# First phase of an attention and gated-layer kernel: weights made without ScalarE, and five of eight w3 row tiles moved into the first gated layer

## The chip, the cores and the metric

The kernel runs on one core of a Trainium2 chip. A core has TensorE (matrix products, PE in the profile; its weight loads are PEld), VectorE (DVE), ScalarE (ACT), GpSimd (POOL) and SyncE (SP), whose queue issues all DMA transfers here. The metric is device time in microseconds (us): the median of several runs. Less is better. One profiled execution gives the trace that the rows below come from.

## What is computed

```python
attn_out = sigmoid(q @ k.T / sqrt(64) - log(448)) @ v     # 4 batches, 12 heads, 448 rows, 64 columns
x = attn_out as (1792, 768)
xn = x / rms(x) * rms_g
x  = (silu(xn @ w_gate) * (xn @ w_val)) @ w_out           # first gated layer, width 1536
y  = ((x @ w1) * (x @ w2)) @ w3 @ w_out2                  # second layer, width 1024
```

The weights arrive as 64-bit floats. On the chip each is turned into a 32-bit float and then split into a rounded high part and the rest (both in TensorE's fp32r format), so that every large product is three matmuls.

## The kernel before

**Attention.** The 12 heads of a batch are worked in 6 pairs; pairs 0 to 11 (batches 0 and 1) make up the first phase, and pairs 12 to 23 are spread through the layers that follow. `load_pair` brings one pair's rows (q, k and v, 736 KB, tile `raw`, 3 buffers), `scores` makes the four score blocks of a pair and applies the sigmoid on ScalarE (tiles `a` and `al`), `attend` multiplies with v into `av`, and `take_out` copies the result to `xr` on ScalarE, writes it to DRAM, squares it on ScalarE and adds the square to `acc` on GpSimd. In the order of TensorE's instructions, pair i's scores stand between the products of pair i-1.

**Weights.** `load_double` brings a 64-bit tile (`wd`). `to_float` decodes it: `mag` is the high word without its sign (ScalarE, L96), VectorE clamps it (L97), shifts it (L98), and joins sign and low word (L106, L109) to the float `wf`. `split_weight` copies `wf` to the high part on ScalarE (L115) and subtracts on GpSimd (L116). Two sets of weights are made in the first phase: the eight tiles of the last weight, w_out2, which stay on chip as `o0` to `o7` (`load_wo2`, `decode_wo2`, one per pair), and the first row tiles of w3. Class `Weights` holds all others in one sequence; at most two loaded tiles (`wd`, 2 buffers) wait for decoding, two decoded ones (`wf`, 2 buffers) for splitting, and four split ones (`ws`) for TensorE.

**w3 @ w_out2.** `w3o_group(kt, nh)` makes one half of one row tile of this product, 24 matmuls of 384 columns, and writes it to DRAM through `w3ot`. Before the change all 8 row tiles (16 groups, 16 weight tiles of 512 columns) are made between the first 12 pairs and the first gated layer. Meanwhile `rms_norm(b)` makes the factor `r` of a batch, and `split_x(b, k)` reads x back from DRAM, scales it (`xs`, L385) and splits it (`x`, ScalarE L262, VectorE L263).

**First gated layer.** For each of 12 column tiles m and both batches, `a_group` makes the gate product and the value product: 18 matmuls of 448 columns each, into one of three PSUM tiles `psm`. The gate's sigmoid is on ScalarE, the two multiplications by it are on VectorE (L491, L495), and they free the PSUM tiles. Two weight tiles of 768 columns (wg and wv) are needed per m. A scheduler in the framework sets the order of each engine's queue once, before the run; within a queue the order is fixed, so an instruction that waits holds all behind it. All DMAs stand in SyncE's queue.

Of the kernel before, what the change touches and what calls it, by code (L numbers as in the profile page):

```python
# [8 lines left out]
F32 = mybir.dt.float32  # L9
# [27 lines left out]
def fused_kernel(ctx: ExitStack, tc: tile.TileContext, qkv, wg, wv, wo, w1, w2, w3, wo2, gam, out):  # L37
# [80 lines left out]
    class Weights:  # L118
# [57 lines left out]

        def split_to(self, n, flush=False):

            n = min(n, len(self.seq) - 1)
            while self.n_split <= n and len(self.split) < self.BUFS:  # L180
# [5 lines left out]
                if double:  # L186
                    f = to_float(f, w)
# [7 lines left out]
                if kt is None:  # L195
                    for j in range(2):
                        split_weight(t[:, :, j * WH : (j + 1) * WH], next(self.blocks), WH)
                elif double:
                    self.late = (i, t, f, w)
                else:  # L200
                    split_weight(t, f, w)
                    self.out -= 1
            if flush:
                self.finish()

# [15 lines left out]
    W = Weights()  # L221
    i_w3 = [[W.add(w3[kt][:, 4 * h : 4 * h + 4, :], 4, True) for h in range(2)] for kt in range(KF2)]
    kept = {}
# [11 lines left out]
    B_ORDER = [0, 3, 1, 4, 2, 5]  # L235
    i_a = [[add_moe(n, w, m) for n, w in (("wg", wg), ("wv", wv))] for m in range(KF1)]
    i_b = {m: [add_moe("wo", wo, m, h) for h in range(2)] for m in range(KD)}
# [59 lines left out]

    A1 = dict(raw=3, a=5, al=2, xr=2, wd=2)
    A2 = dict(raw=2, a=3, al=2, xr=2)
# [6 lines left out]
    xd = {}  # L306

    def load_pair(p):
        if p < NP:
            t = raw[p] = at([P, RAWW], F32, "raw")  # L310

            cuts = (0, S + P, V0, RAWW) if p == 0 else (0, RAWW)
            for c, d in zip(cuts, cuts[1:]):
                nc.sync.dma_start(out=t[:, c:d], in_=qkv[p // HP, p % HP][:, c:d])

# [29 lines left out]
    def take_out(p):  # L345
# [36 lines left out]
    def load_x(b, k):  # L382
        x = scratch("xs")
        nc.sync.dma_start(out=x, in_=xd.pop((b, k)))
        nc.vector.scalar_tensor_tensor(  # L385
            out=x, in0=x, scalar=g_sb[:, k : k + 1], in1=rms[b], op0=ALU.mult, op1=ALU.mult
        )
        return x

    def split_x(b, k):  # L390
        t = x_tile("x", b % 2)
        split2(t, load_x(b, k))
        acts["x", b % 2, k] = t

# [65 lines left out]
    def a_winograd(m):  # L460
        def done(b, g, v):
# [9 lines left out]
    def c_winograd(m):  # L471
        def done(b, x, y):
            nc.vector.tensor_tensor(out=y, in0=x, in1=y, op=ALU.mult)
            acts["ab", b, m] = t = h_tile("ab")
            split2(t, y)

        winograd(i_c2, m, done)


    def h_tile(name):  # L480
        return pools["h"].tile([P, 2, S], F32R, tag="h", bufs=2 * KF1, name=name)

    half = {}

    def a_group(m, b, which):
# [25 lines left out]
    def c_group(m, b, which):  # L511
# [6 lines left out]
        else:  # L518
            s = half.pop((m, b))
            nc.vector.tensor_tensor(out=s, in0=ps, in1=s, op=ALU.mult)  # L520
            t = h_tile("ab")
            split2(t, s)
# [42 lines left out]
    load_pair(0)  # L565
    load_wo2(0)
    load_pair(1)
    load_wo2(1)
    load_pair(2)
    for i in range(NA + 1):  # L570
        if i < NA:
# [3 lines left out]
        if i:  # L575
            attend(i - 1, (3, 0))
        if i < KF2:
            decode_wo2(i)
            load_wo2(i + 2)
# [7 lines left out]
        if i >= KF2 - 1:  # L587
            W.load_to(i - KF2 + 2)
            W.split_to(i - KF2)
        if i == HP:  # L590
            rms_norm(0)
        if i > HP and i - HP <= KD:
            split_x(0, i - HP - 1)


    groups = [(kt, nh) for kt in range(KF2) for nh in range(2)]
    for n, g in enumerate(groups):
        w3o_group(*g)
        W.split_to(n + 4)
        if n == 1:  # L600
            rms_norm(1)
        if n > 3 and n - 4 < KD:
            split_x(1, n - 4)
    att["pool"].release()
    wo2p.release()
    att["pool"], att["bufs"] = pool("att2", "left"), A2
    pools["h"] = pool("h", "right")

# [13 lines left out]

    steps = [lambda: (load_pair(NA), load_pair(NA + 1))]
    for p in range(NA, NP):
# [3 lines left out]
    steps += [lambda: first_half(NP), lambda: None, lambda: rms_norm(B - 1)]  # L628
    units = list(first_units())
    total = sum(u[1] for u in units)  # L630
    spent, n = 0.0, len(steps)
    for u in units:
        spent += run(u)
        while steps and (n - len(steps)) < n * spent / total:
            steps.pop(0)()
    assert not steps
# [21 lines left out]
    pools["xw"].release()  # L658
    pools["h"].release()
    for p in (r1b, wp, scr, r1a, cst, ps_w, ps_av, ps_m, dram):  # L660
        p.release()
# [53 lines left out]
```

## Time and profile before

| what | value |
| --- | --- |
| median of 3 runs | 1138.17 us (1137.58 to 1139.41) |
| the profiled execution's own time | 1137.84 us |
| its span, first to last instruction | 1136.1 us |
| TensorE busy | 1101.1 us (97%) |
| VectorE, ScalarE, GpSimd busy | 643.5, 471.8, 371.8 us |
| mean granted TensorE clock | 0.991 of full speed |

The span is what the rows are measured in; 1.7 us of the execution's own time lie around it. A busy time of VectorE or GpSimd includes time in which an instruction has started and is held. Matmuls are pipelined: the duration of one is longer than the distance to the next, so the pace is read from starts.

### The profile page before, as it was taken

How to read it: one execution, taken by the hardware profiler on the slowest of the kernel's cores; microseconds unless marked ns; L12 is line 12 of the kernel's file. 1: busy time of each engine (PE TensorE's matmuls, PEld its weight loads, DVE VectorE, ACT ScalarE, POOL GpSimd, SP SyncE). 2: the span in 40 equal slices, each digit the busy share in tenths (PEclk: the TensorE clock that was granted, in tenths of full speed). 3: DMA queues.
4: the chain of work that ended last, by engine and by line, in shares of the span. 5: the costliest groups of instructions: out<-in, count | busy, mean ns of one | idle time of the engine just before them, and what ended most of it. 6: DMA issues, size and time to landing. Idle time of an engine off the chain costs nothing.

```text
span 1136.1 us, 13921 instructions
## 1 busy us (share of the span) xinstructions
PE 1101.1 (97%) x5204; PEld 904.1 (80%) x5204; DVE 643.5 (57%) x873; ACT 471.8 (42%) x768; POOL 371.8 (33%) x276
## 2 busy tenths in 40 slices
PE   7779997899999999999999999999999999999998
PEld 2223997777887788787778899999889999899997
DVE  5662677764656565343544365599999222777600
ACT  6766443444344443434433233544443233433321
POOL 2421232121222222131212213556565222556420
PEclk9889999999999999999999999999999999999999
DMA  8554556544344453644433225211112110121131
GB/s 285 193 189 136 170 187 234 192 160 160 133 153 171 148 179 106 201 153 167 161 125 126 93 88 165 102 56 56 56 56 86 55 56 19 56 69 44 38 103 51
DMA packets 55218, 141.41 MB, mean 124 GB/s; under 512 B 5232, under 2 KB 28912, under 8 KB 55152
## 3 DMA queue, kind: packets, MB, share of 16 engines
q1 hardware_dynamic: 55152, 140.53, 36.6%
q8 instruction: 41, 0.67, 0.2%
q14 instruction: 25, 0.20, 0.1%
HBM read 105.91 MB, written 34.60 MB: 124 GB/s over the span
## 4 chain that ended last, share of the span: by engine, by line
PE 84%; DVE 7%; DMA 4%; ACT 2%; issue 1%; POOL 1%; SPq 0%; DVEq 0%; ACTq 0%; POOLq 0%
PE psm L247 17%; PE psm L248 16%; PE psm L249 16%; PE w L247 8%; PE w L248 7%; PE w L249 7%; PE av L343 4%; PE sc L325 4%; DMA wd<-in_wg 2%; DVE wf L106 2%; DVE wf L109 2%; PE psm L328 1%; PE av L339 1%; DVE wf L98 1%; DVE mag L97 1%
## 5 line engine op out<-in xcount | busy, mean ns | idle before, releaser
L116 POOL TENSOR_TENSOR ws<-wf,ws 128x768 fp32r<-128x768 f32 (+1 forms) x104 | 173.9, 1674 | 489.6 <-ACT ws L115 459.4
L247 PE MATMUL w<-w,ws 128*128 128x448 f32 x420 | 154.8, 369 | 1.5 <-ACT w L262 1.5
L248 PE MATMUL w<-w,ws 128*128 128x448 f32 x420 | 154.4, 368 | 0.0
L249 PE MATMUL w<-w,ws 128*128 128x448 f32 x420 | 154.0, 367 | 0.0
L96 ACT ACTIVATE mag<-wd 128x768 f32<-128x768 f32 (+1 forms) x76 | 65.6, 863 | 173.5 <-DVE wf L98 73.5
L247 PE MATMUL psm<-x,ws 128*128 128x448 f32 x288 | 109.4, 380 | 9.5 <-ACT w3ot L292 5.7
L98 DVE TENSOR_SCALAR wf<-mag 128x768 uint32<-128x768 uint32 (+1 forms) x76 | 45.5, 598 | 111.4 <-POOL ws L116 109.2
L116 POOL TENSOR_TENSOR ws<-wd,ws 128x384 fp32r<-128x384 f32 x80 | 87.7, 1112 | 60.8 <-ACT ws L115 60.8
L247 PE MATMUL psm<-hm,ws 128*128 128x448 f32 x288 | 107.4, 373 | 0.0
L248 PE MATMUL psm<-x,ws 128*128 128x448 f32 x288 | 106.2, 369 | 0.0
L249 PE MATMUL psm<-x,ws 128*128 128x448 f32 x288 | 106.0, 368 | 0.0
L115 ACT ACTIVATE ws<-wf 128x768 fp32r<-128x768 f32 (+1 forms) x104 | 78.7, 758 | 65.5 <-PE psm L249 43.4
L248 PE MATMUL psm<-hm,ws 128*128 128x448 f32 x288 | 105.6, 367 | 0.0
L249 PE MATMUL psm<-hm,ws 128*128 128x448 f32 x288 | 104.8, 364 | 0.0
L116 POOL TENSOR_TENSOR ws<-s,ws 128x384 fp32r<-128x384 f32 x60 | 71.1, 1189 | 63.8 <-ACT ws L115 62.1
L325 PE MATMUL sc<-raw 64*128 64x448 f32 x288 | 73.6, 603 | 14.9 <-DMA raw<-in_qkv 9.0
L247 PEld LDWEIGHTS w<-w,ws 128*128 128x128 f32 x420 | 78.7, 188 | 10.9 <-ACT w L262 1.8
L109 DVE SCALAR_TENSOR_TENSOR wf<-wd,wf 128x768 uint32<-128x768 uint32 (+1 forms) x76 | 85.4, 1123 | 1.4
L97 DVE TENSOR_SCALAR mag<-mag 128x768 f32<-128x768 f32 (+1 forms) x76 | 44.3, 583 | 73.7 <-ACT mag L96 73.7
L106 DVE SCALAR_TENSOR_TENSOR wf<-wd,wf 128x768 uint32<-128x768 uint32 (+1 forms) x76 | 84.4, 1110 | 2.5
L249 PEld LDWEIGHTS w<-w,ws 128*128 128x128 f32 x420 | 78.9, 188 | 7.7
L248 PEld LDWEIGHTS w<-w,ws 128*128 128x128 f32 x420 | 78.8, 188 | 7.3
(118 smaller groups left out, 2160.2 us busy)
## 6 DMA issues: line engine op xcount, KB each, us to landing
raw<-in_qkv SPq DMA_DIRECT2D x23, 736.0 KB, 5.3
wd<-in_wo SPq DMA_DIRECT2D x20, 768.0 KB, 5.2
wd<-in_w SPq DMA_DIRECT2D x16, 768.0 KB, 4.5
wd<-in_wg SPq DMA_DIRECT2D x12, 768.0 KB, 4.6
wd<-in_wv SPq DMA_DIRECT2D x12, 768.0 KB, 5.5
wd<-in_w SPq DMA_DIRECT2D x16, 512.0 KB, 4.0
w<-wf SPq DMA_DIRECT2D x16, 384.0 KB, 2.5
wf<-w3o SPq DMA_DIRECT2D x24, 256.0 KB, 2.8
```

Source lines behind the costliest of these rows:

```text
L96: nc.scalar.activation(mag, hi.bitcast(F32), AF.Abs)
L97: nc.vector.tensor_scalar(out=mag, in0=mag, scalar1=HI_MIN, scalar2=HI_MAX, op0=ALU.max, op1=ALU.min)
L98: nc.vector.tensor_scalar(out=u, in0=mag.bitcast(U32), scalar1=3, scalar2=0x3FFFFFFF, op0=ALU.logical_shift_left, op1=ALU.bitwise_and,)
L106: nc.vector.scalar_tensor_tensor(out=u, in0=hi, scalar=0xC0000000, in1=u, op0=ALU.bitwise_and, op1=ALU.bitwise_or)
L109: nc.vector.scalar_tensor_tensor(out=u, in0=lo, scalar=29, in1=u, op0=ALU.logical_shift_right, op1=ALU.bitwise_or)
L115: nc.scalar.activation(t[:, 0, :w], f[:, :w], AF.Copy)
L116: nc.gpsimd.tensor_tensor(out=t[:, 1, :w], in0=f[:, :w], in1=t[:, 0, :w], op=ALU.subtract)
L247: nc.tensor.matmul(ps, wl, xt[:, 0, :], start=first, stop=False)
L248: nc.tensor.matmul(ps, wh, xt[:, 1, :], start=False, stop=False)
L249: nc.tensor.matmul(ps, wh, xt[:, 0, :], start=False, stop=last)
L325: nc.tensor.matmul(ps[:, j, :], r[d, k], r[d, Q0 : Q0 + S], start=True, stop=True)
L343: nc.tensor.matmul(av[p][d, :], r[:, v + j * D : v + (j + 1) * D], a[:, j, :], start=False, stop=(c == 2))
```

## The change

- The eight tiles of w_out2 and the first six half tiles of w3 are decoded and split without ScalarE: `mag` is made on VectorE (a bitwise AND, one more VectorE operation per tile), and the high part on GpSimd (a copy, CAST, one more GpSimd operation per tile).
- Loads of these weights stand behind the load of the next pair's rows in SyncE's queue (`issue_after`), and each decode comes at the end of its pair, one pair later than before.
- x of batches 0 and 1 stays on chip (8 buffers of `xr`): 12 writes to DRAM and 12 reads fall away. `split_x` works one tile ahead.
- Only row tiles 0 to 2 of w3 @ w_out2 come between the 12 pairs and the gated layer. Row tiles 3 to 7 follow the first five column tiles m of the gated layer, one each, and the weight sequence is ordered to match. The second half's attention begins after m = 5.

```diff
+W3_FIRST = 3
...
-    def to_float(raw, w):
+    def to_float(raw, w, scalar=True):
...
-        nc.scalar.activation(mag, hi.bitcast(F32), AF.Abs)
+        if scalar:
+            nc.scalar.activation(mag, hi.bitcast(F32), AF.Abs)
+        else:
+            nc.vector.tensor_scalar(
+                out=mag.bitcast(U32), in0=hi, scalar1=0x7FFFFFFF, scalar2=None, op0=ALU.bitwise_and
+            )
...
-    def split_weight(t, f, w):
-        nc.scalar.activation(t[:, 0, :w], f[:, :w], AF.Copy)
+    def split_weight(t, f, w, scalar=True):
+        if scalar:
+            nc.scalar.activation(t[:, 0, :w], f[:, :w], AF.Copy)
+        else:
+            nc.gpsimd.tensor_copy(out=t[:, 0, :w], in_=f[:, :w])
...
+                    f = to_float(f, w, i >= 2 * W3_FIRST)
...
+    for kt in range(W3_FIRST):
+        add_w3(kt)
+    for m in range(KF1):
+        i_a.append([add_moe(n, w, m) for n, w in (("wg", wg), ("wv", wv))])
+        if W3_FIRST + m < KF2:
+            add_w3(W3_FIRST + m)
...
     def decode_wo2(j):
-        f = to_float(raw2.pop(j), DM)
-        W.finish()
+        f = to_float(raw2.pop(j), DM, False)
         t = wo2p.tile([P, 2, DM], F32R, tag=f"o{j}", name=f"o{j}")
-        W.late = (None, t, f, DM)
+        split_weight(t, f, DM, False)
         o2.append(t)
...
-    A1 = dict(raw=3, a=5, al=2, xr=2, wd=2)
+    A1 = dict(raw=3, a=5, al=2, xr=8, wd=2)
...
-        d = xd[b, h] = dram.tile([P, S], F32, name=f"x{b}_{h}")
-        nc.sync.dma_start(out=d, in_=x)
+        if p < NA:
+            xd[b, h] = x
+        else:
+            d = xd[b, h] = dram.tile([P, S], F32, name=f"x{b}_{h}")
+            nc.sync.dma_start(out=d, in_=x)
...
+    DECODE = {1: 0, 2: 1, 3: 2, 4: 3, 5: 4, 6: 5, 7: 6, 8: 7}
+    W3_AT = {6: 0, 8: 1, 9: 2, 10: 3, 11: 4, 12: 5}
...
+        with tc.issue_after(last_raw[0]):
+            if i in DECODE:
+                decode_wo2(DECODE[i])
+                load_wo2(DECODE[i] + 2)
+            if i in W3_AT:
+                W.load_to(W3_AT[i] + 1)
+                W.split_to(W3_AT[i] - 1)
...
+    def w3o_groups(kt):
+        for nh in range(2):
+            w3o_group(kt, nh)
+            W.split_to(i_w3[kt][1] + 2 + nh)
+            W.load_to(i_w3[kt][1] + 4 + nh)
+
+    w3o_groups(0)
+    rms_norm(1)
+    for k in range(KD + 1):
+        if k % 3 == 2:
+            w3o_groups(k // 3 + 1)
+        split_x(1, k)
...
+    half_a = 4 * (KF1 // 2)
+    for j, u in enumerate(units[:half_a]):
+        run(u)
+        if j % 4 == 3 and len(i_w3) > W3_FIRST + j // 4:
+            w3o_groups(W3_FIRST + j // 4)
```

On ScalarE, these rows before the change stand in the third pair of the first phase (L96 and L115 are the weights' two operations, L330 the sigmoids, L349 the copy of a pair's result):

```order
L330 ACTIVATE a_222<-sc_221,bias_s_88 128x896
L96 ACTIVATE mag_256<-wd_184 128x768
L349 ACTIVATE xr_230<-av_205 128x448
L115 ACTIVATE o1_218<-wf_210 128x768
L354 ACTIVATE acc_234<-xr_230 128x448
L330 ACTIVATE a_239<-sc_238,bias_s_88 128x896
L330 ACTIVATE a_244<-sc_243,bias_s_88 128x896
L330 ACTIVATE al_249<-psm_248,bias_s_88 128x448
L96 ACTIVATE mag_304<-wd_219 128x768
L115 ACTIVATE o2_265<-wf_257 128x768
L330 ACTIVATE a_269<-sc_268,bias_s_88 128x896
```

The same place of ScalarE's queue in the changed kernel (L349 is the sigmoid there, L368 the copy, L376 and L379 the squares):

```order
L349 ACTIVATE a_200<-sc_199,bias_s_88 128x896
L368 ACTIVATE xr_208<-av_195 128x448
L376 ACTIVATE acc_210<-xr_208 128x448
L349 ACTIVATE a_227<-sc_226,bias_s_88 128x896
L349 ACTIVATE a_232<-sc_231,bias_s_88 128x896
L349 ACTIVATE al_237<-psm_236,bias_s_88 128x448
L349 ACTIVATE a_245<-sc_244,bias_s_88 128x896
```

The weights' rows are gone from ScalarE's queue between the sigmoids.

On GpSimd, before the change, the first phase begins with (o0, o1, ... are the tiles of w_out2, acc the sum of squares):

```order
L116 TENSOR_TENSOR o0_183<-wf_177,o0_183 128x768
L116 TENSOR_TENSOR o1_218<-wf_210,o1_218 128x768
L116 TENSOR_TENSOR o2_265<-wf_257,o2_265 128x768
L116 TENSOR_TENSOR o3_313<-wf_305,o3_313 128x768
L358 TENSOR_TENSOR acc_234<-acc_234,sq_281 128x448
L116 TENSOR_TENSOR o4_361<-wf_353,o4_361 128x768
```

In the changed kernel GpSimd has at the same place:

```order
L126 CAST o0_221<-wf_215 128x768
L127 ISA
L127 TENSOR_TENSOR o0_221<-wf_215,o0_221 128x768
L126 CAST o1_267<-wf_261 128x768
L127 TENSOR_TENSOR o1_267<-wf_261,o1_267 128x768
L380 TENSOR_TENSOR acc_210<-acc_210,sq_255 128x448
L126 CAST o2_313<-wf_307 128x768
L127 TENSOR_TENSOR o2_313<-wf_307,o2_313 128x768
```

Each tile now has a CAST ahead of its subtraction, and the sum of squares of pair 1 stands behind the split of tile 1, that of pair 2 behind tile 2.

On VectorE, the changed kernel reaches the first gate multiplication (L521, which frees the first PSUM tile of the gated layer) in this order; the rows ahead of it are the last halves of a w3 tile (mag_1115, wf_1116), the last x tiles of batch 1 (xs, x) and the whole decode of the second wg tile (mag_1152, wf_1153):

```order
L105 TENSOR_SCALAR mag_1115<-mag_1115 128x512
L281 TENSOR_TENSOR x_1012<-xs_924,x_1012 128x448
L410 SCALAR_TENSOR_TENSOR xs_1010<-xr_731,g_sb_86,r_817 128x448
L106 TENSOR_SCALAR wf_1116<-mag_1115 128x512
L114 SCALAR_TENSOR_TENSOR wf_1116<-wd_968,wf_1116 128x512
L281 TENSOR_TENSOR x_1015<-xs_1010,x_1015 128x448
L117 SCALAR_TENSOR_TENSOR wf_1116<-wd_968,wf_1116 128x512
L105 TENSOR_SCALAR mag_1152<-mag_1152 128x768
L106 TENSOR_SCALAR wf_1153<-mag_1152 128x768
L114 SCALAR_TENSOR_TENSOR wf_1153<-wd_1008,wf_1153 128x768
L117 SCALAR_TENSOR_TENSOR wf_1153<-wd_1008,wf_1153 128x768
L521 TENSOR_TENSOR s_1041<-psm_1022,s_1041 128x448
```

Before the change the rows ahead of the first gate multiplication are decodes of wg and wv alone, since x and w3 are done by then:

```order
L97 TENSOR_SCALAR mag_1627<-mag_1627 128x768
L98 TENSOR_SCALAR wf_1628<-mag_1627 128x768
L106 SCALAR_TENSOR_TENSOR wf_1628<-wd_1521,wf_1628 128x768
L109 SCALAR_TENSOR_TENSOR wf_1628<-wd_1521,wf_1628 128x768
L491 TENSOR_TENSOR s_1491<-psm_1472,s_1491 128x448
```

The work on x and on w3 that used to lie ahead of the gated layer now shares VectorE's queue with its first column tile.

## Rows read from the trace of the kernel before

**Rows 1.** First line of the profile's page.
```profile
span 1136.1 us, 13921 instructions
```

**Rows 2.** Busy time by stage: stretch, length, then each engine's busy us, clock, DMA.
```profile
17.90:85.00 67.10, 52.58 (x172) 16.52 (x170) 47.71 (x52) 45.80 (x63) 26.85 (x17) 0.87 0.61 210
85.00:113.20 28.20, 28.05 (x114) 9.23 (x112) 6.59 (x11) 19.68 (x29) 3.40 (x3) 1.00 0.42 137
113.20:184.80 71.60, 71.28 (x402) 67.90 (x400) 49.23 (x69) 29.07 (x51) 21.30 (x15) 1.00 0.57 187
184.80:230.00 45.20, 35.77 (x159) 29.34 (x159) 31.31 (x37) 19.20 (x27) 10.99 (x6) 0.96 0.58 197
230.00:1136.10 906.10, 901.13 (x4323) 777.00 (x4321) 502.36 (x694) 347.38 (x587) 308.07 (x231) 1.00 0.32 106
```

**Rows 3.** Timeline of TensorE: start, us, instruction; starts of pairs and of w3 @ w_out2.
```profile
17.94 1.77 PE L325 MATMUL sc<-raw 64*128 64x448 f32 x8
...
85.04 1.77 PE L325 MATMUL sc<-raw 64*128 64x448 f32 x8
...
91.95 1.77 PE L325 MATMUL sc<-raw 64*128 64x448 f32 x8
...
113.22 0.44 PE L288 MATMUL psm<-o,ws 128*128 128x384 f32 x1
```

**Rows 4.** The chain that ended last, first phase: start, us, what.
```profile
23.29 0.95 ACT mag L96
...
25.53 2.46 DVE wf L106
...
29.00 0.84 ACT o L115
```

**Rows 5.** Timeline of VectorE, a decode of 768 columns with nothing in its way.
```profile
10.82 0.56 DVE L97 TENSOR_SCALAR mag<-mag 128x768 f32<-128x768 f32 x1 [9.80 <-ACT mag L96]
...
13.00 0.96 DVE L109 SCALAR_TENSOR_TENSOR wf<-wd,wf 128x768 uint32<-128x768 uint32 x1
```

**Rows 6.** Timeline, GpSimd and VectorE at the same time, 512 columns.
```profile
155.60 1.30 POOL L116 TENSOR_TENSOR ws<-wf,ws 128x512 fp32r<-128x512 f32 x1 [0.43 <-ACT ws L115]
155.66 1.78 DVE L106 SCALAR_TENSOR_TENSOR wf<-wd,wf 128x512 uint32<-128x512 uint32 x1
157.90 0.68 DVE L109 SCALAR_TENSOR_TENSOR wf<-wd,wf 128x512 uint32<-128x512 uint32 x1
```

**Rows 7.** Instructions of the w_out2 tiles: ns min/median/max, first and last start.
```profile
L116 POOL TENSOR_TENSOR o<-wf,o x8: 1809/1856/2634, 16.9 to 54.7; 128x768 fp32r<-128x768 f32 x8
```

**Rows 8.** Groups of GpSimd (85 to 113.2) and VectorE (to 203.3): busy, mean ns, idle.
```profile
L358 POOL TENSOR_TENSOR acc<-acc,sq 128x448 f32<-128x448 f32 x3 | 3.4, 1133 | 32.4 <-ACT sq L357 32.4
...
L385 DVE SCALAR_TENSOR_TENSOR xs<-xs,g_sb,r 128x448 f32<-128x448 f32 x12 | 8.2, 682 | 25.4 <-DMA xs<-x 25.4
L263 DVE TENSOR_TENSOR x<-xs,x 128x448 fp32r<-128x448 f32 x12 | 7.8, 651 | 4.0 <-ACT x L262 3.9
```

**Rows 9.** Timeline of TensorE, matmuls of w3 @ w_out2 without a pause between.
```profile
172.30 0.34 PE L289 MATMUL psm<-o,ws 128*128 128x384 f32 x1
...
184.43 0.34 PE L290 MATMUL psm<-o,ws 128*128 128x384 f32 x1
```

**Rows 10.** Timeline of TensorE, first products of the gated layer, with idle time before.
```profile
198.43 0.47 PE L247 MATMUL psm<-x,ws 128*128 128x448 f32 x1 [3.56 <-ACT w3ot L292]
...
203.75 0.37 PE L247 MATMUL psm<-x,ws 128*128 128x448 f32 x1
...
224.50 0.47 PE L247 MATMUL psm<-x,ws 128*128 128x448 f32 x1 [3.60 <-DVE s L491]
...
228.07 0.36 PE L249 MATMUL psm<-x,ws 128*128 128x448 f32 x1
```

**Rows 11.** DMA issues: KB each, median us from issue to landing.
```profile
wd<-in_wg SPq DMA_DIRECT2D x12, 768.0 KB, 4.6
...
wd<-in_w SPq DMA_DIRECT2D x16, 512.0 KB, 4.0
```

More of the change, by code (lines that the diff above doesn't have):

```diff
@@ L198, in split_to @@
                 elif double:
-                    self.late = (i, t, f, w)
+                    self.late = (i, t, f, w, i >= 2 * W3_FIRST)
                 else:
@@ L202, in split_to @@
                     self.out -= 1
-            if flush:
-                self.finish()
         def finish(self):
@@ L221, in fused_kernel, with add_w3 @@
     W = Weights()
-    i_w3 = [[W.add(w3[kt][:, 4 * h : 4 * h + 4, :], 4, True) for h in range(2)] for kt in range(KF2)]
+    i_w3, i_a = [], []
+    def add_w3(kt):
+        i_w3.append([W.add(w3[kt][:, 4 * h : 4 * h + 4, :], 4, True) for h in range(2)])
     kept = {}
@@ L306, in fused_kernel @@
     xd = {}
+    last_raw = []
     def load_pair(p):
@@ L313, in load_pair @@
             for c, d in zip(cuts, cuts[1:]):
-                nc.sync.dma_start(out=t[:, c:d], in_=qkv[p // HP, p % HP][:, c:d])
+                last_raw[:] = [nc.sync.dma_start(out=t[:, c:d], in_=qkv[p // HP, p % HP][:, c:d]).ins]
     def scores(p, c):
@@ L383, in load_x @@
         x = scratch("xs")
-        nc.sync.dma_start(out=x, in_=xd.pop((b, k)))
+        y = xd.pop((b, k))
+        if b > 1:
+            nc.sync.dma_start(out=x, in_=y)
+            y = x
         nc.vector.scalar_tensor_tensor(
-            out=x, in0=x, scalar=g_sb[:, k : k + 1], in1=rms[b], op0=ALU.mult, op1=ALU.mult
+            out=x, in0=y, scalar=g_sb[:, k : k + 1], in1=rms[b], op0=ALU.mult, op1=ALU.mult
         )
         return x
+    ready = []
     def split_x(b, k):
-        t = x_tile("x", b % 2)
-        split2(t, load_x(b, k))
-        acts["x", b % 2, k] = t
+        if k < KD:
+            ready.append(load_x(b, k))
+        if k:
+            t = acts["x", b, k - 1] = x_tile("x", b)
+            split2(t, ready.pop(0))
     def right_tile(name, bl):
@@ L473, in done, with h_tile @@
             nc.vector.tensor_tensor(out=y, in0=x, in1=y, op=ALU.mult)
-            acts["ab", b, m] = t = h_tile("ab")
+            acts["ab", b, m] = t = h_tile("ab", m)
             split2(t, y)
         winograd(i_c2, m, done)
-    def h_tile(name):
-        return pools["h"].tile([P, 2, S], F32R, tag="h", bufs=2 * KF1, name=name)
+    def h_tile(name, m):
+        return pools[f"h{int(m >= KF1 // 2)}"].tile([P, 2, S], F32R, tag="h", bufs=KF1, name=name)
     half = {}
@@ L565, in fused_kernel @@
     load_pair(0)
-    load_wo2(0)
     load_pair(1)
-    load_wo2(1)
+    with tc.issue_after(last_raw[0]):
+        load_wo2(0)
     load_pair(2)
+    with tc.issue_after(last_raw[0]):
+        load_wo2(1)
+    DECODE = {1: 0, 2: 1, 3: 2, 4: 3, 5: 4, 6: 5, 7: 6, 8: 7}
+    W3_AT = {6: 0, 8: 1, 9: 2, 10: 3, 11: 4, 12: 5}
     for i in range(NA + 1):
@@ L586, in fused_kernel @@
                 load_pair(i + 2)
-        if i >= KF2 - 1:
-            W.load_to(i - KF2 + 2)
-            W.split_to(i - KF2)
+        with tc.issue_after(last_raw[0]):
+            if i in DECODE:
[4 more added lines that the diff above has]
+                W.split_to(W3_AT[i] - 1)
         if i == HP:
             rms_norm(0)
-        if i > HP and i - HP <= KD:
+        if i > HP:
             split_x(0, i - HP - 1)
[L596 to L603, printed above, removed]
+    split_x(0, KD)
+    def w3o_groups(kt):
[9 more added lines that the diff above has]
+        split_x(1, k)
     att["pool"].release()
-    wo2p.release()
-    att["pool"], att["bufs"] = pool("att2", "left"), A2
-    pools["h"] = pool("h", "right")
+    pools["h0"] = pool("h0", "left")
+    steps = []
     def first_half(p):
@@ L621, in second_half @@
         scores(p, 3)
-    steps = [lambda: (load_pair(NA), load_pair(NA + 1))]
+    steps.append(lambda: (load_pair(NA), load_pair(NA + 1)))
     for p in range(NA, NP):
@@ L629, in fused_kernel @@
     units = list(first_units())
+    half_a = 4 * (KF1 // 2)
[3 more added lines that the diff above has]
+            w3o_groups(W3_FIRST + j // 4)
+    wo2p.release()
+    att["pool"], att["bufs"] = pool("att2", "left"), A2
+    pools["h1"] = pool("h1", "right")
+    units = units[half_a:]
     total = sum(u[1] for u in units)
@@ L632, in fused_kernel @@
     for u in units:
+        while steps and (n - len(steps)) <= n * spent / total:
+            steps.pop(0)()
         spent += run(u)
-        while steps and (n - len(steps)) < n * spent / total:
-            steps.pop(0)()
+    while steps:
+        steps.pop(0)()
     assert not steps
@@ L658, in fused_kernel @@
     pools["xw"].release()
-    pools["h"].release()
-    for p in (r1b, wp, scr, r1a, cst, ps_w, ps_av, ps_m, dram):
+    pools["h1"].release()
+    for p in (pools["h0"], r1b, wp, scr, r1a, cst, ps_w, ps_av, ps_m, dram):
         p.release()
```

13 lines of the change are left out of this document (4 added, 9 removed).

## Prediction

> **What bounds the kernel now.** I read the busy times by stage first. From 230 us on TensorE is busy 901.1 of 906.1 us at full clock [rows 2]; nothing in the first phase can help there, and the edits leave that work as it is. What can be won lies ahead of 230 us. Between 17.9 and 85.0 us TensorE is busy only 52.6 of 67.1 us, at a granted clock of 0.87; between 85.0 and 113.2 it is busy 28.05 of 28.20 at 1.00 [rows 2]. Both stretches do the same thing, pairs of heads. The starts of pairs give the sizes: undisturbed, one pair takes 91.95 - 85.04 = 6.91 us; from 17.94 to 85.04 only six pairs are worked, which needs 41.5 us and took 67.1 [rows 3]. So some 25 us are lost there. The chain of waits names the cause: a weight's decode passes from ScalarE to VectorE and back to ScalarE, where it stands in one queue with the sigmoids that TensorE needs [rows 4]. In the stretch without a loss ScalarE has no such work left.
>
> The second loss is at the start of the gated layer: 45.2 us from 184.8 on, with 35.8 busy [rows 2]. TensorE waits 3.56 us at 198.43 and 3.60 us at 224.50 [rows 10], and 18 matmuls from 198.43 on take 5.32 us, where 17 steps from 224.50 to 228.07 take 3.57, 3.8 for 18: the granted clock of that stretch is 0.96 on the mean, since a part of it ran at 1.2 instead of 2.4 GHz after the wait.
>
> **If TensorE alone set the pace.** As a mark I take the start of the fourth product of the gated layer, where before it stood at 203.75 [rows 10]. After the change the path to it is: pair 2 starts at 17.94 as before; ten more pair periods, 69.1; the product of the root mean square, 1; the last pair's products with v, half a period, 3.4; six groups of w3 @ w_out2; three products of 3.8 us, 11.4. A group is 24 matmuls; 71 rows from 172.30 to 184.43 [rows 9] are 0.173 us apart, so a group is 4.16 us and six are 25.0. Sum: 128. From the mark on, the old kernel needs 1136.1 - 203.75 = 932.4 us, of which 3.6 are the wait at 224.50; the new one adds ten groups, 41.6. So the end is mark + 970.4 + new waits. With a mark of 128 and none, the span is 1098.4.
>
> **What the edits cost, part by part.** ScalarE loses two operations per tile, which is the 25 us above; that is not free, because both go to engines that hinder each other. At 155.60 GpSimd's subtraction starts, 0.06 us later VectorE's L106, and this takes 1.78 us where the same-sized L109 behind it takes 0.68: it stood still until GpSimd was done [rows 6]. In the first stretch their busy times add up to 47.7 + 26.9 = 74.6 in 67.1 us, holding included [rows 2]. So I count both engines' work as one sum, up to the first gate multiplication (L521 in the changed order), which the fourth product needs because the three PSUM tiles are full.
>
> VectorE: a decode of 768 columns is 2 x 0.56 + 2 x 0.96 = 3.04 us (L98 as L97, L106 as L109 [rows 5]); eleven of them are 33.4. The added AND takes a word from every second place; nearest is L97 at 0.56 (bounds 0 to L109's 0.96), eight times 4.5. Decodes of 512 columns are two thirds of the 0.56 twice, and 0.68 twice [rows 6], 2.1; eight are 16.8, and six ANDs 2.2. The twelve x tiles are 8.2 + 7.8 = 16.0 [rows 8]. The short steps of two root mean squares, eight at some 0.6, are 4.8 (an estimate from the x rows). Sum 77.7. GpSimd: eight subtractions at 1.81 [rows 7], 14.5; two for wg and wv, 3.6; eight of 512 columns at 1.30 [rows 6], 10.4; ten sums of squares at 1.13 [rows 8], 11.3. Sum 39.8. The new CASTs are in no row: eight of 768 columns and six of 512, as much as twelve large ones. One can cost from nothing to the 1.81 of the subtraction, which reads two tiles where the CAST reads one; I take half, 0.9, so 10.8 (0 to 21.7). All together 128.3.
>
> By the Trainium skill (GPSIMD Engine Reference, 3.1 Elementwise), a one-input body on GpSimd goes at 1.03 cycles per element and two-input arithmetic at 2.6, and ordinary elementwise work is better left to VectorE. At the page's clock that makes a CAST some 0.8 us, an estimate, and the sum 1 us less; no run so far shows one.
>
> The first w_out2 tile lands by 9.9 us now, as its decode begins at 10.82 behind ScalarE's 0.9 [rows 4, 5]. A pair's rows now go ahead of it; I put it at 12. If the two engines never pause, the mark is reached at 12 + 128 = 140, and 12 us after TensorE could be there. For handovers between them I add 5: mark 145. Seventeen microseconds of waiting then stand ahead of the mark, most of it at the third and fourth product.
>
> The loads cost SyncE's queue nothing that shows: a tile behind a pair's rows waits for the decode two tiles back, and if it does, the next pair's rows wait behind it, but that decode has two pair periods for itself. The dropped x transfers free VectorE's 25.4 us of waiting for `xs` [rows 8], which hid beside TensorE's w3 groups and is no gain by itself. The sum of squares of pair 5 now stands behind a tile's split on GpSimd, so the root mean square's product comes some 3 us late; that lies ahead of the mark and beside the sum, so I add nothing.
>
> **In the gated layer** each of five steps m is four products (15.2) and two groups (8.3), 23.5 us, and needs four weight tiles. One load buffer passes a large tile and a small one per step: 4.6 + 0.9 + 3.04 and 4.0 + 0.7 + 2.1 [rows 4, 5, 6, 11], 15.3, with some 4 for GpSimd's operations in between, 19 of 23.5. So supply is enough if nothing stands in its way. But a gate multiplication stands behind decodes in VectorE's queue, and a decode behind its load, as the wait of 3.60 before 224.50 shows [rows 10]. Bounds: 0, and five times 3.6, 18. I take 1.6 each, 8. One or two slow-clock stretches like that at 198.43 add 2.
>
> **Sum.** 145 + 970.4 + 8 + 2 = 1125.4 of span, against 1136.1 [rows 1]. The profiled execution has 1.7 us around its span and is 0.3 below the median, so the forecast is 1127 us, 11 less than before.
>
> **Rivals.**
> - *VectorE and GpSimd keep up.* Both idle much between 85 and 113 us now (6.6 and 3.4 of 28.2 us busy [rows 2]), and that room is used. If a CAST is short and most GpSimd work falls into VectorE's pauses, the mark is near 130 and the steps lose 2: 130 + 970.4 + 2 + 1.7 = 1104. Against it: the held L106 [rows 6]. The skill (SBUF — State Buffer, Who interferes with whom) calls the shared port an exclusive lock for the whole instruction; by that rule this rival is out unless the sum itself is smaller. Chance 0.22.
> - *The CAST costs as much as the subtraction.* The sum grows by 10.9, the mark moves to 156, and the time to 1138: no change. For it: both write the same rounded tile. Against it: one operand less. Chance 0.15.
> - *Slower: the steps of the gated layer become bound by their weights.* Place: the load of the next wg, which waits for the decode of a w3 tile, which waits for a split that ScalarE makes only behind a gate sigmoid. If that circle takes 29 us instead of 19, each of five steps loses 5.5 us, 28 in all: 145 + 970.4 + 28 + 1.7 = 1145. It decides from some 19 us of waits in the steps on. For it: one such wait in the old kernel's short time at the layer's start [rows 10]; against it: none after 224.50, with two tiles per step. Chance 0.13.
>
> **How the numbers follow.** The forecast's case has the rest, 0.50; its own range is 1115 to 1139, from a mark of 138 to 154 and steps that lose 3 to 13. Over all cases I give 1104 to 1142: below lies half of the first rival, above it most of the last. The runs before lie within 0.16%, so I take 0.2%, 2.3 us, as no change. Faster: most of the forecast's case (0.48), the first rival, and nearly half of the second: 0.76. Same: 0.07. Slower: the last rival, and the rest of the second: 0.17.
>
> **What would show it.** Right: pairs 2 to 11 at about 6.9 us, w3 @ w_out2 begun near 90 us, VectorE and GpSimd without a common pause from 12 to 145 us, TensorE waiting for VectorE ahead of the fourth product, and small waits in each of the five steps. A CAST near 0.9 us, an AND near 0.6. Wrong: a fourth product near 130 us (the sum is too large), pairs that wait for their rows (the queue), CASTs near 2 us, or waits above 4 us in each step.

## The result, and the profile after

The changed kernel takes 1122.41 us (median of 4 runs, 1121.15 to 1124.76), the kernel before 1137.99 beside it (1137.58 to 1139.41): ratio 0.9863, 95% interval 0.9845 to 0.9882, so some 15.6 us less. The forecast was 1127 with a range of 1104 to 1142. The first line of the page after:

```profile
span 1119.3 us, 13869 instructions
```

The same stretches as in [rows 2], of the changed kernel (stretch, length, then busy us of TensorE, its weight loads, VectorE, ScalarE and GpSimd, TensorE's granted clock, DMA):

```profile
17.90:85.00 67.10, 63.34 (x244) 21.34 (x242) 50.78 (x55) 43.61 (x59) 33.94 (x26) 0.97 0.55 194
85.00:113.20 28.20, 26.10 (x120) 15.64 (x117) 21.91 (x30) 13.25 (x20) 12.71 (x11) 0.94 0.38 129
113.20:184.80 71.60, 65.94 (x348) 62.12 (x347) 56.64 (x78) 27.16 (x45) 18.19 (x11) 1.00 0.50 162
184.80:230.00 45.20, 43.58 (x228) 40.89 (x227) 25.74 (x43) 16.85 (x28) 12.75 (x8) 1.00 0.49 152
```

TensorE is now busy 63.3 of the first 67.1 us, where it was 52.6, at a granted clock of 0.97 of full speed instead of 0.87. Between 85 and 113 us, where nothing was lost before, it now loses 2.1 us, and VectorE, which had 6.6 us of work there, has 21.9. TensorE's own timeline answers to [rows 3] and [rows 10] (start, duration, instruction, idle time before it and what ended it):

```profile
17.55 1.77 PE L344 MATMUL sc<-raw 64*128 64x448 f32 x8
24.46 1.02 PE L344 MATMUL sc<-raw 64*128 64x448 f32 x4
...
54.99 1.02 PE L386 MATMUL psm<-acc,ones 128*128 128x448 f32 x2 [1.11 <-POOL acc L380]
...
69.01 1.77 PE L344 MATMUL sc<-raw 64*128 64x448 f32 x8
...
76.05 1.02 PE L344 MATMUL sc<-raw 64*128 64x448 f32 x4 [2.66 <-ACT a L349]
77.00 3.20 PE L362 MATMUL av<-a,raw 128*64 128x448 f32 x8
...
93.69 1.44 PE L344 MATMUL sc<-raw 64*128 64x448 f32 x4 [2.10 <-ACT a L349]
...
97.94 0.44 PE L305 MATMUL psm<-o,ws 128*128 128x384 f32 x1
...
128.72 0.44 PE L265 MATMUL psm<-x,ws 128*128 128x448 f32 x1 [1.39 <-ACT w3ot L309]
...
141.57 0.47 PE L265 MATMUL psm<-x,ws 128*128 128x448 f32 x1 [1.66 <-DVE s L521]
...
167.58 0.47 PE L265 MATMUL psm<-x,ws 128*128 128x448 f32 x1 [2.61 <-DVE s L521]
```

Pairs start 24.46 - 17.55 = 6.91 us apart. At 54.99 the first norm's product waits for a sum of squares on GpSimd. Two of the later pairs wait for a sigmoid, and eight products with v behind the first such wait take 3.20 us, where they take 1.72 undisturbed: the granted clock of that stretch is 0.52, the lower of the two levels. w3 @ w_out2 begins at 97.94 (before at 113.22), the gated layer's first product at 128.72, and the fourth, the prediction's mark, at 141.57. From the mark to the end are 1119.3 - 141.57 = 977.7 us.

What holds the sigmoid at 76 us stands in the timelines of ScalarE and then of VectorE, 72 to 87 us:

```profile
74.52 0.58 ACT L280 ACTIVATE x<-xs 128x448 fp32r<-128x448 f32 x1 [4.18 <-DVE xs L410]
75.01 1.89 ACT L349 ACTIVATE a<-sc,bias_s 128x896 f32<-128x896 f32 x2
```

```profile
72.81 1.68 DVE L410 SCALAR_TENSOR_TENSOR xs<-xr,g_sb,r 128x448 f32<-128x448 f32 x1
...
81.95 1.20 DVE L281 TENSOR_TENSOR x<-xs,x 128x448 fp32r<-128x448 f32 x1 [4.19 <-ACT x L280]
86.35 0.43 DVE L102 TENSOR_SCALAR mag<-wd 128x512 uint32<-128x512 uint32 x1 [3.20 <-DMA wd<-in_w]
```

ScalarE waits 4.18 us for an xs that stands behind a decode in VectorE's queue, and the sigmoid stands behind that split of x in ScalarE's. Right after, VectorE itself idles 4.19 and 3.20 us. So neither engine was short of time here; the order of the work made the wait.

### The profile page after: what moved, and what is told of

Same layout as the page of the kernel before. It is cut to its first block, busy times and chain, and to the rows that moved or that the text cites. A ratio compares the mean times of both kernels' runs of the same rounds, so it can differ in the third digit from the quotient of the medians.

```text
span 1119.3 us, 13869 instructions
## 1 busy us (share of the span) xinstructions
PE 1095.3 (98%) x5204; PEld 902.1 (81%) x5204; DVE 652.9 (58%) x887; ACT 452.0 (40%) x740; POOL 387.6 (35%) x290
## 4 chain that ended last, share of the span: by engine, by line
PE 78%; DVE 10%; DMA 6%; ACT 2%; POOL 2%; issue 1%; SPq 0%; DVEq 0%; ACTq 0%; POOLq 0%
PE psm L265 15%; PE psm L266 14%; PE psm L267 14%; PE w L265 8%; PE w L266 8%; PE w L267 8%; PE av L362 4%; PE sc L344 4%; DMA wd<-in_wg 3%; DVE wf L114 2%; POOL ws L127 2%; DMA wd<-in_w 2%; DVE wf L117 2%; PE psm L347 1%; DVE mag L105 1%
## 5 line engine op out<-in xcount | busy, mean ns | idle before, releaser
L100 ACT ACTIVATE mag<-wd 128x768 f32<-128x768 f32 (+1 forms) x62 | 53.9, 869 | 175.9 <-DVE wf L106 54.4
L106 DVE TENSOR_SCALAR wf<-mag 128x768 uint32<-128x768 uint32 (+1 forms) x76 | 49.9, 656 | 114.0 <-POOL ws L127 112.3
L265 PE MATMUL psm<-x,ws 128*128 128x448 f32 x288 | 107.7, 374 | 8.3 <-DVE s L521 6.8
L267 PE MATMUL psm<-x,ws 128*128 128x448 f32 x288 | 105.3, 366 | 0.0
L266 PE MATMUL psm<-x,ws 128*128 128x448 f32 x288 | 105.3, 366 | 0.0
L124 ACT ACTIVATE ws<-wf 128x768 fp32r<-128x768 f32 (+1 forms) x98 | 74.8, 766 | 56.8 <-PE psm L267 42.1
L265 PEld LDWEIGHTS w<-w,ws 128*128 128x128 f32 x420 | 78.7, 188 | 10.8 <-ACT w L280 1.8
L117 DVE SCALAR_TENSOR_TENSOR wf<-wd,wf 128x768 uint32<-128x768 uint32 (+1 forms) x76 | 84.7, 1114 | 1.4
L344 PE MATMUL sc<-raw 64*128 64x448 f32 x288 | 70.3, 587 | 9.7 <-ACT a L349 5.1
L349 ACT ACTIVATE a<-sc,bias_s 128x896 f32<-128x896 f32 x72 | 70.1, 1000 | 21.0 <-PE sc L344 20.9
```

The costliest lines, as they stand in the source:

```text
L106: nc.vector.tensor_scalar(out=u, in0=mag.bitcast(U32), scalar1=3, scalar2=0x3FFFFFFF, op0=ALU.logical_shift_left, op1=ALU.bitwise_and,)
L117: nc.vector.scalar_tensor_tensor(out=u, in0=lo, scalar=29, in1=u, op0=ALU.logical_shift_right, op1=ALU.bitwise_or)
L265: nc.tensor.matmul(ps, wl, xt[:, 0, :], start=first, stop=False)
L266: nc.tensor.matmul(ps, wh, xt[:, 1, :], start=False, stop=False)
L267: nc.tensor.matmul(ps, wh, xt[:, 0, :], start=False, stop=last)
L344: nc.tensor.matmul(ps[:, j, :], r[d, k], r[d, Q0 : Q0 + S], start=True, stop=True)
```

## The experiments

All are timed beside the kernel before on their own chip, which took 1138.98 to 1139.27 us there, so ratios are compared; a thousandth is 1.14 us. "Mark" is the start of the fourth product. Two theories stood against each other: **A**, the prediction's, that the summed work of VectorE and GpSimd sets the mark; **B**, that queues do: what stands in ScalarE's or SyncE's queue behind something that waits.

| kernel | ratio, interval | mark | span less mark |
|---|---|---|---|
| changed | 0.9863 (0.9845 to 0.9882) | 141.57 | 977.7 |
| cast_twice | 0.9875 (0.9860 to 0.9890) | 144.66 | 978.4 |
| high_part_on_scalar | 0.9864 (0.9831 to 0.9897) | 142.18 | 978.9 |
| magnitude_on_scalar | 0.9914 (0.9887 to 0.9940) | 151.83 | 978.7 |
| weights_with_scalar | 0.9918 (0.9900 to 0.9935) | 149.42 | 978.6 |
| loads_not_behind_rows | 1.0018 (1.0005 to 1.0030) | 159.76 | 978.7 |
| loads_behind_rows_only | 0.9955 (0.9938 to 0.9973) | another order | |
| x_through_dram | 0.9867 (0.9844 to 0.9891) | 143.65 | 980.3 |
| w3_all_first | 0.9888 (0.9870 to 0.9906) | another order | |
| x_split_behind_sigmoids | 0.9834 (0.9810 to 0.9859) | 138.40 | 978.1 |
| last_sums_first | 0.9826 (0.9802 to 0.9849) | 139.62 | 981.5 |
| last_sums_first_2 | 0.9811 (0.9795 to 0.9827) | 136.56 | 979.5 |
| second_norm_first | 0.9807 (0.9792 to 0.9823) | 136.67 | 978.3 |

Marks and spans are those of the profiled execution, ratios those of all. The last column moves by less than 4 us, the mark by 23: most of what was done to the first phase was decided by the time of the mark.

**cast_twice** doubles the suspected work:

```diff
             nc.gpsimd.tensor_copy(out=t[:, 0, :w], in_=f[:, :w])
+            nc.gpsimd.tensor_copy(out=t[:, 0, :w], in_=f[:, :w])
```

> The changed kernel with each of GpSimd's 14 CASTs of the first phase done twice (8 tiles of 768 columns, 6 of 512). In the changed kernel they take 0.82 and 0.61 us at the least, 0.95 and 0.74 on the mean, so 10 to 12 us are added to the work of GpSimd and VectorE together. Theory A (the summed work of the two engines sets when the fourth product of the gated layer can start, now at 141.6 us): the fourth product moves to 151 to 154 and the time to 1132 to 1135. Theory B (the two engines have room; what is late is late because ScalarE's queue holds a sigmoid behind a split of x that waits for VectorE): the fourth product moves by 0 to 4 us, the time is 1122 to 1127.

The second copies, by groups of GpSimd from 12 to 142 us (busy us, mean ns, idle before):

```profile
L127 POOL CAST o<-wf 128x768 fp32r<-128x768 f32 x8 | 7.9, 989 | 0.5
...
L127 POOL CAST ws<-wf 128x512 fp32r<-128x512 f32 x6 | 4.1, 690 | 0.4
```

They add 12.0 us, holding included, and the mark moves by 3.1. A, as a sum from 12 us on, is out: most of what is added falls into pauses.

**high_part_on_scalar** and **magnitude_on_scalar** bring back one of ScalarE's two operations each, **weights_with_scalar** both:

```diff
-        if scalar:
+        if True:
             nc.scalar.activation(mag, hi.bitcast(F32), AF.Abs)
...
-        if scalar:
+        if True:
             nc.scalar.activation(t[:, 0, :w], f[:, :w], AF.Copy)
```

> The changed kernel with the high part of the early weights' split on ScalarE again (14 copies, GpSimd's CASTs go), the magnitude stays on VectorE. Theory A (sum of VectorE and GpSimd): 10 to 12 us less work for the two, so the fourth product of the gated layer comes earlier and the time is 1112 to 1118. Theory B (ScalarE's queue): each copy waits for the end of a decode on VectorE while sigmoids stand behind it, so this operation alone carries most of what the run with both operations on ScalarE lost: 1126 to 1131.

> The changed kernel with the magnitude of the early weights on ScalarE again; the high part stays with GpSimd's CASTs. With both on ScalarE the time was 1130, with the high part alone 1122. Theory M (the magnitude costs, since it waits for a load's landing with sigmoids behind it): 1127 to 1131. Theory C (the circle costs: a copy that waits for a decode that waits for a magnitude behind sigmoids in the same queue, so that only both together lose): 1120 to 1124.

> The changed kernel with one part undone: each weight's magnitude and high part come from ScalarE again, for the w_out2 tiles and the first w3 tiles as well. The loads behind the rows, x on chip and the moved row tiles stay. Theory A and the prediction's first step: the decode passes through ScalarE's queue again and the pairs from 17.9 us on lose up to 25 us; since 13 to 14 us are waited ahead of the fourth product anyway, the fourth product comes 5 to 15 us later and the time is 1128 to 1137. Rival: the order of the work (tiles spread over pairs, five row tiles moved) made the gain alone, and the sum of VectorE and GpSimd falls by 17 us when ScalarE takes these steps: the time is 1115 to 1122.

The high part alone moves nothing, and so misses both expectations: not A's, though all 14 CASTs (12.4 us) are gone from GpSimd, nor B's, though ScalarE does wait for decodes. The magnitude alone costs 0.0051, 5.8 us, as much as both together (0.0055). ScalarE's waits from 12 to 139 us (waited for: us in total, times, longest), first of the run with the high part, then of that with the magnitude:

```profile
ACT o L124 <- DVE wf L117: 11.5, 6, 2.2
```

```profile
ACT mag L100 <- DMA wd<-in_wo: 10.8, 7, 2.6
ACT mag L100 <- DMA wd<-in_w: 10.3, 3, 5.0
```

A w_out2 copy waits 2.2 us at the most for its decode. The magnitude waits 21.1 us for loads; 5.0 of that is one wait at 129 us, of a tile that ScalarE decodes in the changed kernel too, which leaves 16.1 us, 3.2 at the longest. The total does not measure the loss: with both operations on ScalarE the magnitude waits only 10.2 us for loads, and the time is the same. Where the loss falls can be read. In the run with the magnitude, ScalarE and then TensorE do this in the last pair:

```profile
104.16 0.66 ACT L100 ACTIVATE mag<-wd 128x512 f32<-128x512 f32 x1 [3.18 <-DMA wd<-in_w]
104.72 1.00 ACT L349 ACTIVATE a<-sc,bias_s 128x896 f32<-128x896 f32 x1
105.61 0.54 ACT L368 ACTIVATE xr<-av 128x448 f32<-128x448 f32 x1
```

```profile
106.21 1.86 PE L358 MATMUL av<-al,raw 128*128 128x448 f32 x2 [3.60 <-ACT xr L368]
```

The copy xr, which frees TensorE's output tile, stands behind a magnitude that waits for its load; TensorE waits 3.60 us for it and then works at a granted clock of 0.51 until 112 us. With both operations on ScalarE TensorE waits 5.18 us for the same copy (103.68), and the clock is 0.53 until 110; with the high part alone it waits 1.28 us (99.31). That the magnitude is the part that costs is shown; that it costs by holding what stands behind it is argued from these rows.

**loads_not_behind_rows** takes the three blocks away that queue loads behind the rows; **loads_behind_rows_only** gives the kernel before these alone, with the loads of w_out2 and of the first w3 tiles moved behind the pair's rows:

```diff
...
-        with tc.issue_after(last_raw[0]):
+        if True:
             if i in DECODE:
                 decode_wo2(DECODE[i])
...
```

```diff
...
             if i + 2 < NA:
                 load_pair(i + 2)
...
+        with tc.issue_after(last_raw[0]):
+            if i < KF2:
+                load_wo2(i + 2)
...
```

> The changed kernel with one part undone: the weights' loads are not held behind the pairs' rows on SyncE's queue, so a weight's load that waits for its buffer stands ahead of a pair's rows. If that order matters, TensorE waits for raw in the pairs, some 1 to 2 us at three or four pairs as before the change, with stretches at the lower clock behind: first phase 4 to 10 us longer, time 1124 to 1131. If it does not (the rows have two pair periods to land), the time is 1120 to 1124.

> The kernel before with one part of the change alone: each weight's load stands behind the pairs' rows on SyncE's queue. Weights with ScalarE, x through DRAM and all row tiles ahead of the gated layer stay as before. Theory L (what the pairs lost was rows that came late behind a weight's load, and what followed from it): TensorE's waits for raw go, the pairs get 10 to 15 us shorter and the time is 1123 to 1129. Theory W (the prediction's first step: what the pairs lost was the decode in ScalarE's queue with the sigmoids): TensorE waits for sigmoids as before and the time is 1133 to 1138.

The first loses the whole gain, 0.0155 or 17.6 us, well beyond the 4 to 10 us that were expected. TensorE's and SyncE's waits, 12 to 147 and 10 to 110 us, of that run:

```profile
PE sc L344 <- DMA raw<-in_qkv: 16.0, 3, 9.9
```

```profile
SPq L90 <- DVE wf L117: 33.1, 8, 5.6
...
SPq L90 <- DVE mag L105: 16.3, 1, 16.3
```

Weights' loads wait 33.1 and 16.3 us for a decode to free their buffer, and the rows behind them come late: TensorE waits up to 9.9 us for raw. This is not the order of before, which had 4.4 us of such waits in four places; without ScalarE in the decode, the scheduler put two loads ahead of a row at several places, and on VectorE all 14 early tiles are decoded ahead of the first norm, where the changed kernel has 7 of them there. The 17.6 us are the price of that whole order. Alone, the edit is worth 0.0045, 5 us, the size that theory W gave: TensorE's waits for raw vanish, as theory L said, but those for ScalarE stay (12 to 113 us):

```profile
PE sc L326 <- ACT a L331: 5.0, 5, 1.9
PE av L340 <- ACT xr L350: 4.3, 1, 4.3
```

So the order of loads is what the other edits, taken together, need to be worth anything, more than it is a gain of its own.

**x_through_dram** and **w3_all_first** undo the other two parts:

```diff
-        if p < NA:
+        if False:
             xd[b, h] = x
...
-        if b > 1:
+        if True:
             nc.sync.dma_start(out=x, in_=y)
```

> The changed kernel with one part undone: x of all pairs goes through DRAM again before the norm's gain is applied. The prediction's step: those transfers hid beside TensorE's work and give no gain by themselves, so the time is that of the changed kernel, 1120 to 1125. Rival: an xs in VectorE's queue that waits for its landing holds decodes and, through the split on ScalarE, sigmoids too; then 1126 to 1132.

```diff
-W3_FIRST = 3
+W3_FIRST = 8
...
         split_x(1, k)
+    for kt in range(3, W3_FIRST):
+        w3o_groups(kt)
```

> The changed kernel with all eight row tiles of w3 @ w_out2 ahead of the gated layer; the other parts stay. Ten groups (41.6 us of TensorE) come back ahead of the fourth product, and 10 tiles of 512 columns for VectorE and GpSimd with them, about 45 us. Theory A: the fourth product starts near 190 and the rest takes 929, so the span is about 1121 and the time the same as with five tiles moved (1120 to 1124). Theory B: the fourth product starts at 141.6 + 41.6 = 183 or earlier, since waits ahead of it are filled, and the steps of the gated layer lose nothing: span 1110 to 1114, time 1112 to 1116, faster than the changed kernel.

x on chip is worth nothing that shows (0.9867). The five row tiles are worth 0.0025, 2.8 us, in median; the intervals overlap, so the size is uncertain and neither theory's number came. The rows show where it would lie: with all tiles first, ScalarE and TensorE do this at 160 us:

```profile
159.85 0.90 ACT L100 ACTIVATE mag<-wd 128x768 f32<-128x768 f32 x1 [11.72 <-DMA wd<-in_wg]
...
164.81 0.86 ACT L309 ACTIVATE w3ot<-psm 128x384 f32<-128x384 f32 x2
```

```profile
165.44 0.66 PE L305 MATMUL psm<-o,ws 128*128 128x384 f32 x1 [5.24 <-ACT w3ot L309]
```

The same pattern: a magnitude waits 11.72 us for its load, an eviction stands behind it, TensorE waits 5.24 us for the PSUM tile.

**x_split_behind_sigmoids** puts each split of x behind the next pair's sigmoids in ScalarE's queue (VectorE's rows of those tiles move back with it; no work is added):

```diff
...
         if i < NA:
             scores(i, 2)
+        if i > HP + 1:
+            with tc.issue_after(last_sig[0]):
+                split_x(0, i - HP - 2)
...
```

> The changed kernel, but in the pairs the copy of a split of x stands behind the four sigmoids of the next pair in ScalarE's queue, not ahead of them. No work is added or taken away. Theory B (queue): the waits of TensorE of 2.66 us at 76.05 and 2.10 us at 93.69 go, and with them the products at the lower clock behind them; the fourth product starts near 134 and the time is some 1115. Theory A (sum of VectorE and GpSimd): the pairs go on without those waits, but the wait is found again ahead of the third and fourth product; the fourth product starts at 140 to 142 and the time is 1120 to 1123.

The two waits go and the last pair's second scores stand at 87.76 instead of 93.69, 5.9 us earlier; at the mark 3.2 of it are left, and the time is 0.0029, some 3 us, lower. Both theories get a part: the pairs were held by the queue, but half of what they gain is lost again before the mark. TensorE now waits 2.20 us for the last sum of squares and works at a granted clock of 0.69 behind it, until 110 us, and the first product waits 1.78 us where it was 1.39:

```profile
104.53 1.02 PE L386 MATMUL psm<-acc,ones 128*128 128x448 f32 x2 [2.20 <-POOL acc L380]
125.55 0.44 PE L265 MATMUL psm<-x,ws 128*128 128x448 f32 x1 [1.78 <-ACT w3ot L309]
```

**last_sums_first** and **last_sums_first_2** build on this edit and were to remove the first of these waits. In the first only pair 10's sums moved; those of pair 11 still stood behind a magnitude that waited 8.70 us for its load, the norm's product came at 105.74, and the run decides nothing. The second also covers the later groups and the last splits:

```diff
-            nc.scalar.activation(sq, x, AF.Square)
+            last_sig[:] = [nc.scalar.activation(sq, x, AF.Square).ins]
...
-    w3o_groups(0)
-    rms_norm(1)
-    for k in range(KD + 1):
+    with tc.issue_after(last_sig[0]):
+        w3o_groups(0)
+        rms_norm(1)
+        for k in range(KD + 1):
...
```

(In the first only `w3o_groups(0)` stands in the block.)

> As the run with the split of x behind the sigmoids, and the last pair's copy and square stand ahead of the magnitude of the first wg tile in ScalarE's queue (there that magnitude waited 8.97 us for its load with the copy and square behind it, and TensorE then 2.20 us for the sum of squares). No work is added or taken away. Theory B: the product of the second root mean square, at 104.53 in that run, comes at 98 to 100, the first product of the gated layer at 121 to 123 where it was 125.55, the fourth at 134 to 136, the time is 1115 to 1117. Theory A: the fourth product stays at 138 and the time at 1119 to 1120.

> As the run with the split of x behind the sigmoids, and the copy and square of the last pair, number 11, stand ahead of the first wg tile's magnitude and of the splits of x in ScalarE's queue; in the earlier attempt the edit had moved only those of pair 10. Theory B: the product of the second root mean square comes at 97 to 101 where it was 104.5, the first product of the gated layer at 121 to 123 where it was 125.5, and the time is 1113 to 1116. Rival: the first product waits for VectorE, which decodes the first wg and wv tiles in the same stretch and takes 10 us for the second root mean square, whenever its sums come; it stays at 125 to 126 and the time at 1118 to 1120.

Now the sum is there at 97 us, but the first product comes at 124.82, the mark at 136.56; with 1118.27 us it is the rival's case by time. **second_norm_first** then puts the second norm ahead of the last splits of x and of the decodes of wg and wv (`last_sig` holds its square root in the second block):

```diff
+    with tc.issue_after(last_sig[0]):
+        w3o_groups(0)
+        with tc.issue_after(group_end[0]):
+            rms_norm(1)
+    with tc.issue_after(last_sig[0]):
+        split_x(0, KD - 1)
...
```

> As the run before with the last pair's sums first, and the second root mean square stands ahead of what followed it badly there: its product behind the first group of w3 @ w_out2, its square root on ScalarE ahead of the last splits of x of the first batch and of the magnitudes of wg and wv, its chain on VectorE ahead of their decode. No work is added or taken away. If ScalarE's and VectorE's order in 98 to 122 us sets the first product of the gated layer (124.8 in that run, where the square root came only at 109.5 though the sums were there at 97), the square root comes near 100 to 102, the first product at 119 to 122, the fourth, which then finds its gate multiplication done, at 130 to 133, and the time is 1111 to 1115. Rival: the decodes of wg and wv that now stand behind make the first product wait for its weights, or the two engines' summed work is the bound after all: first product 124 to 126, time 1117 to 1120.

TensorE's first two products of the gated layer, and the busy times from 104 to 128 us, of that run:

```profile
118.53 0.36 PE L265 MATMUL psm<-x,ws 128*128 128x448 f32 x1
...
127.49 0.74 PE L265 MATMUL psm<-x,ws 128*128 128x448 f32 x1 [5.14 <-POOL ws L127]
```

```profile
104.00:128.00 24.00, 18.86 (x104) 18.23 (x103) 23.98 (x34) 11.23 (x19) 4.07 (x2) 0.93 0.32 110
```

The first product comes 10 us earlier than in the changed kernel and without a wait; the second then waits 5.14 us for wv, whose decode was put back, and the mark is where it was, 136.67. VectorE is busy 23.98 of 24.00 us, GpSimd 4.07. So VectorE's work looks like the bound of this stretch, and the order only chooses who waits for it; no run takes work away from it there, which would show it. This is the lowest ratio of all, 0.9807, some 6 us below the changed kernel; from last_sums_first_2 it can't be told apart.

## Why the prediction was right, and where it was not

**The pairs at 6.91 us: right up to pair 7.** Pairs 2 to 7 start 6.91 us apart. Pair 8 starts 9.98 us after pair 7: the first norm's product lies between them, and TensorE waits 1.11 us for its sum of squares, the wait for which the prediction added nothing. Pair 10 starts 11.12 us after pair 9, and pair 11 has a wait of 2.10 us. This brought the start of w3 @ w_out2 to 97.94 and not near 90. The last two places were not foreseen: I had taken ScalarE's queue as cured, while a split of x that waits for VectorE holds a sigmoid there as well.

**The cause of the 25 us: half right.** TensorE idled 67.10 - 52.58 = 14.5 of them [rows 2]; the rest was work at a lower clock. The step "a weight's decode passes from ScalarE to VectorE and back to ScalarE" blamed the whole circle. In the changed order the magnitude carries the loss; the way back costs nothing that shows. And the step "the loads cost SyncE's queue nothing that shows" put the new order at nothing either way: undone, it costs 17.6 us. I had priced what the loads' new place costs, and not what it would cost if they stayed.

**TensorE alone: near.** Its first product was forecast at 128 less three of 3.8, 116.6; in second_norm_first it started at 118.53.

**The sum of VectorE and GpSimd: near in size, wrong as a mechanism for the whole stretch.** The mark was forecast at 145 and came at 141.57, but of the 17 us of waits ahead of it "most of it at the third and fourth product" 9.3 came: 5.1 for sigmoids in the pairs, with slow products behind, 1.4 at the first product, 1.1 at the norm and only 1.66 at the fourth. The trace shows pauses (VectorE busy 106.48 of the 129.57 us from 12 to the mark, and 3.58 of 11.0 us in the stretch from 76), and 12 us of added work moved the mark by 3. That the mark, and with it the time, came so near the forecast is therefore partly luck: waits and slow products came to 13.6 us beyond TensorE's own path (128), where the sum had put 17 there.

```profile
12.00:141.57 129.57, 120.66 (x520) 62.81 (x516) 106.48 (x126) 72.00 (x103) 56.30 (x42) 0.97 0.48 166
...
76.00:87.00 11.00, 10.95 (x40) 3.53 (x40) 3.58 (x7) 7.23 (x10) 3.40 (x3) 0.84 0.46 163
...
120.00:141.60 21.60, 18.55 (x98) 17.10 (x96) 21.30 (x29) 10.35 (x19) 6.89 (x4) 1.00 0.47 152
```

Only the last stretch is full. There VectorE's work, holding included, seems to bind, since the second norm, x tiles and the decodes of the new order meet.

**The sizes.** Of the terms, the groups after (12 to 142 us; first GpSimd, then VectorE) show:

```profile
L126 POOL CAST o<-wf 128x768 fp32r<-128x768 f32 x8 | 7.6, 946 | 32.9 <-DVE wf L117 32.9
L126 POOL CAST ws<-wf 128x512 fp32r<-128x512 f32 x6 | 4.8, 800 | 13.9 <-DVE wf L117 12.9 <-PE psm L307 0.9
```

```profile
L392 DVE RECIPROCAL r<-t 128x448 f32<-128x448 f32 x2 | 5.9, 2943 | 0.0
...
L395 DVE TENSOR_TENSOR t<-t,v 128x448 f32<-128x448 f32 x2 | 2.9, 1450 | 0.0
```

The CASTs took 7.6 + 4.8 = 12.4 us, holding included, where 10.8 were taken; one of 768 columns takes 0.82 at the least (0.9 forecast), one of 512 columns 0.61, an AND of 768 columns 0.50 to 0.57 undisturbed (0.56 forecast). The Trainium skill (GPSIMD Engine Reference, 3.1 Elementwise) gives 1.03 cycles per element at 1.2 GHz; that is 0.66 us for 768 columns, an estimate, and not the 0.8 that the prediction worked out, so its sum by the page would have been some 3 us less and not 1. Between the two sizes lie 0.21 us for 256 columns, near the 0.22 of the page's rate; a fixed 0.19 us for each CAST comes on top. The two norms were mis-sized: 4.8 us forecast, while two reciprocals alone take 5.9. The same row stands in the trace of before: 2.94 us each.

**The steps of the gated layer: right in size.** Ten us were forecast between the mark and the end beyond 970.4; 977.7 - 970.4 = 7.3 came, in small waits for the gate multiplication (five of 6.8 us in all, that ahead of the mark among them).

**The rivals.** That VectorE and GpSimd keep up was right about the pairs, where cast_twice and high_part_on_scalar show room, and wrong about the last stretch. The xs at 72.81 begins 0.13 us after a GpSimd subtraction of 1.32 us and takes 1.68 us, where its like takes 0.68 [rows 8]. That agrees with the exclusive lock of the Trainium skill (SBUF — State Buffer, Who interferes with whom). But from that rule the prediction had concluded that the rival is out unless the sum is smaller, and in the pairs it was not out: held instructions get longer, and whether the end moves depends on pauses. A CAST as slow as the subtraction, and steps of 29 us, did not come.

## What to carry to other kernels

In an engine that works in order, look for the instruction that waits for a load and count what stands behind it: here the magnitude on ScalarE and the weights' loads on SyncE, each cheap in itself, were worth some 6 and up to 18 us, while 12 us of arithmetic added or taken away cost 1 or nothing. Before two engines' work is summed into a bound, look for the pauses in each stretch by itself; here only the stretch without pauses could be bound by it. And edits that remove waits on the same path need not add up: undone one by one the parts cost 17.6, 5.8, 2.8 and 0.5 us (the last two not clear of the noise), together the change gave 15.6.

## What was not expected of the hardware

A reciprocal of 128x448 on VectorE takes 2.94 us in every one of its four runs, where a multiplication of that size takes 0.62 undisturbed. Of eight ANDs of 768 columns, those at 30.61, 37.35 and 44.28 took 1.09, 1.62 and 2.08 us instead of 0.56. Each began while a subtraction ran on GpSimd (29.46, 36.73 and 44.14, of 1.82, 1.82 and 1.81 us) and ended 0.41 or 0.42 us after it: in these three rows an operation of VectorE waits for the one on GpSimd, although it reads a weight that has just landed and that GpSimd does not touch.
